# Scores of a group's second slab put into the same TensorE step as the first slab's output, clears moved off VectorE, and a new set of planner constants

## The chip, the cores and the metric

The kernel runs on one core of a Trainium2 chip. The metric is the time of one execution in microseconds (us). The kernel before took 628.93 us, the median of three runs (627.5 to 629.05). One profiled execution of it took 627.94 us; its span, from the first to the last recorded instruction, is 625.9 us. All rows below come from that execution.

## The reference

The reference has two stages. The first is a recurrent attention over 768 time steps, for 4 batches of 8 heads of width 48: a 48 x 48 state is multiplied at every step by a complex decay, a key-value product is added, and the query reads the state.

```python
for t in range(S):                       # S = 768
    new_re = ar * S_re - ai * S_im       # ar, ai: normalised decay of this step
    new_im = ar * S_im + ai * S_re
    S_re, S_im = new_re + einsum('bhd,bhe->bhde', k[t], v[t]), new_im
    y[t] = einsum('bhd,bhde->bhe', q[t], S_re)
```

The second is a gated feed-forward network over the 3072 tokens, with 384 model columns and 1536 hidden columns:

```python
g = x @ w_gate
out = (g * sigmoid(g) * (x @ w_val)) @ w_out
```

## The kernel before, in words

**Tiling.** The tokens are cut into 24 slabs of 128 time steps of one batch; two slabs (two batches, the same time steps) are a group, so there are 12 groups. The recurrence over time steps inside a slab is turned into products with cumulated decays. A slab n goes through these steps:

- *Stage* (`stage_ops`, for the whole group): loads, logarithms, exponentials, arctan, sine and cosine on ScalarE, sums over time on TensorE (`cumL`, `cumF`, into the one buffer `pm`), products on VectorE. It ends in the stacks `ks` and `qs`.
- *Turning* (`tr1`, `tr0` on VectorE, line 607, then `sh0` to `sh3`: twelve DMAs issued by SP, line 616): the stacks of a slab are transposed into the tile `T`, which has two buffers. The tile between them, `turned`, has one, so the second slab of a group is turned only when the first one's DMAs are through.
- *Scores* (`sc`, line 641): 64 small matmuls into the two PSUM banks `ps`. They use strips of TensorE, 32 columns wide, each addressed by `tile_position=(0, 32 * slot)`.
- *Mask* (`mk0`, `mk1` on VectorE, line 648), which copies the scores to the tile `sc`.
- *Output and state* (`av`: line 674, 32 or 64 matmuls into `py`, then line 680, 48 matmuls into `pm`): also on strips 32 columns wide. The 48 matmuls of line 680 are left out for the last chunk of time (groups 10 and 11).
- *Eviction* (`evh` on ScalarE, line 698, `evl` on VectorE, line 705): the output becomes the tiles `xh` and `xl` of the group. `ga` and `gm` (VectorE) update the state `G`.

When both slabs of a group are evicted, the feed-forward network of that group runs in 12 steps (`ffn_ops`): line 864 multiplies with the gate and value weights (18 matmuls of 256 columns over the full 128 x 128 array for groups 1 to 11; for group 0 six in single precision, which are 12 records), ScalarE applies silu, VectorE multiplies and splits, and line 903 multiplies with the output weights (6 matmuls of 384 columns).

**Order.** The engines' order of work is written out by a planner (`class Planner`): it goes through the operations by engine, takes an engine that is free first, and among the operations ready at that time the one with the lowest key. A key is a due time, either given (`anchor(n)` for slabs, from `T0`, `LEAD0`, `LEAD2`, `FT0`, `AHEAD`, `PER`; `T0 + f * FT0` and later `T1 + ...` for the feed-forward steps; `CK0`, `X_SEC` for range checks of the inputs) or worked back from the operations that need it, with `STRETCH` times their cost. On ScalarE an operation that needs another table of functions has `SWITCH_KEY` added to its key. `SPARE`, `PIECE` and `CHECK` are added to the landing times that the planner assumes for DMAs, and `QUEUED` says how far ahead of the DMA traffic a load may be issued. The planner's times are assumptions; the engines follow only its order, each in turn, and wait on semaphores.

**Start.** `begin()` comes ahead of the planned order. GpSimd (POOL) makes `ident` twice, once as a triangle, which VectorE copies to `tri` and, turned round by blocks of 32 rows, to its mirror image; VectorE clears the two `vt` tiles and the two `ps` banks, POOL clears `G`. TensorE (PE) is kept busy up to a planned 36 us by matmuls of no use (`p_warm`): ahead of every PE operation stand as many as fit in the planned gap, at 0.3 us each. They stand in PE's queue, in order, so PE runs them all before the operation behind them:

```python
for _ in range(int((min(op.start, WARM) - idle - 0.2) / 0.3)):
    nc.tensor.matmul(out=at_["warm"][:, 0:P], lhsT=mask, rhs=mask, start=True, stop=True)
```

A single-precision matmul is recorded as two, so the 42 records ahead of the first planned PE operation are 21 of these.

Of the kernel before, what the change touches and what calls it, by code (L numbers as in the profile page):

```python
# [17 lines left out]
B, H, S, D = 4, 8, 768, 48  # L18
# [12 lines left out]

SWITCH = 1.273
HOP = 0.145
SWITCH_KEY = 18.625
STRETCH = 1.65
AHEAD, YIELD, QUEUED = -5.599, 3.451, 2.61
T0, PER, FT, FT0 = 21.562, 21.452, 3.64, 4.795
LEAD0, LEAD2 = 15.263, -0.901
CONV0, CONVP = 172.418, 101.298
T1 = T0 + 12 * FT0  # L40
CK0, CKP = 737.912, 29.556
WARM = 36.0
ROW, LAND = 0.6, 2.4
SPARE, PIECE, CHECK = 0.346, 0.281, -0.292
X_SEC = 459.355
RCP, SQR, TURN, SEC = 1, 2, 4, 4
HIGH, LOW, WHOLE = 0, 1, 2
SHY = -80.37
POOL_FROM = 134.7

# [128 lines left out]
def flat(t):  # L181
    return t.rearrange("p h d -> p (h d)")
# [10 lines left out]
def quick(ctx, tc, q, k, v, a_re, a_im, w_gate, w_val, w_out, out, count):  # L193

    nc = tc.nc
# [10 lines left out]
    tri, mirror = masks[:, 0:P], masks[:, P:2 * P]  # L206
    masks = masks.bitcast(F32)
    mask = masks[:, 0:P]
    ident = const.tile([P, P], F32, name="ident")
# [8 lines left out]
    G = const.tile([96, B, H, 64], F32, name="G")  # L218
    vts = [const.tile([P, H + H // 2, 64], F32, name=f"vt{i}") for i in range(2)]
    banks = [psum.tile([P, 512], F32, name=f"p_ps{i}", tag=f"ps{i}", bufs=1) for i in range(2)]  # L220
# [46 lines left out]
    for t, (nm, f, i) in {"re": ("w", 0, 0), "im": ("w", 0, 1), "s1": ("o", 0, 0), "s2": ("w", 1, 0), "s3": ("w", 1, 1),  # L267
                          "qt": ("o", 1, 0), "kt": ("o", 2, 0), "qs": ("w", 2, 0)}.items():
        n, nm_f = 96 if t == "qs" else D, (nm, NF - 3 + f)
# [9 lines left out]
    pl = Planner(slots)  # L279
# [278 lines left out]
                       alloc=[tg(dst)] if opens else [], use=[tg(t), tg(w)] + ([] if opens else [tg(dst)]))  # L558


    def slab_ops(n):
        g, half = divmod(n, 2)
        b, c = where(n)
        N, ta = str(n), anchor(n)
# [3 lines left out]
        made = {st: [f"{st}0_{M}", f"{st}1_{M}"] for st in stacks}  # L568
# [10 lines left out]
        if n < TURN:  # L579
            tdeps = []  # L580
            for i, st in ((1, "ks"), (0, "qs")):
                for hq in range(2):
# [9 lines left out]
                    def ev(e, i=i, hq=hq, inst=inst, first=not tdeps):  # L592
                        if first:
# [4 lines left out]
                                        alloc=[] if tdeps else [("T", n)], use=[("gv", inst)] + ([("T", n)] if tdeps else [])))  # L598
        else:
            halves = [(("bt", 0), f"b{n}"), (("bt", 1), f"b{n}")]  # L600
            bt = tile_t.rearrange("p (j x n) -> p j x n", j=3, x=2)
            for i, st in ((1, "ks"), (0, "qs")):
                def tr(e, i=i, st=st):
                    if i == 1:
# [5 lines left out]
                       alloc=halves if i == 1 else [], use=[stacks[st]] + (halves if i == 0 else []))  # L610
            for i in range(4):
                def sh(e, i=i):
                    if i == 0:
                        new("T", n)
                    for j in range(3):
# [3 lines left out]
                       alloc=[] if i else [("T", n)], use=halves + ([("T", n)] if i else []), lat=1.0 + PIECE, move=0.5)  # L619
            tdeps = [f"sh{i}_{n}" for i in range(4)]  # L620
# [12 lines left out]
        def sc(e):  # L633
            qT, kT = turned(n, 0), turned(n, 1)
            for qd in range(2):
                ps = new("ps", f"{n}.{qd}").rearrange("p (h t) -> p h t", h=4)
                for at, h in ((0, 0), (2, 2), (1, 1), (3, 3)):
                    h = heads[qd][at]
                    for slot in range(4):
                        j = slot if h < H // 2 else 3 - slot  # L640
                        nc.tensor.matmul(out=ps[32 * slot:32 * slot + 32, at, 32 * j:P], lhsT=kT[:, h // 2, h % 2, j, :],  # L641
                                         rhs=qT[:, h // 2, h % 2, j:4, :], start=True, stop=True, tile_position=(0, 32 * slot))
        pl.add("sc" + N, {"PE": 1.35}, sc, deps=tdeps + [f"sc{n - 1}"], alloc=[("ps", f"{n}.0"), ("ps", f"{n}.1")], use=[("T", n)], key=ta)
        for qd in range(2):
            def mk(e, qd=qd):
                s = new("sc", f"{n}.{qd}")
                both = masks.rearrange("p (x t) -> p x t", x=2).unsqueeze(2).to_broadcast([P, 2, 2, P])
                nc.vector.tensor_tensor(out=s.rearrange("p (x h) t -> p x h t", x=2), in0=at_["ps", f"{n}.{qd}"].rearrange("p (x h t) -> p x h t", x=2, h=2),  # L648
                                        in1=both, op=ALU.mult)
            pl.add(f"mk{qd}_{n}", {"DVE": 0.6}, mk, deps=["sc" + N], alloc=[("sc", f"{n}.{qd}")],  # L650
                   use=[("ps", f"{n}.{qd}")])

        def av(e):
            qT, kT = views()
            py = new("py", n)[:, :DM].rearrange("p (k t) -> p k t", k=KT)
            vf, gf = flat(vts[n % 2]), flat(G[:, b])

            turns = [[] for _ in range(4)]
            for blk in range(12):
                pr, j = divmod(blk, 3)  # L660
                slot, kt_ = blk % 4, blk // 4
                o = py[32 * slot:32 * slot + 32, kt_, :]
                heads = ([(2 * pr, 128 * pr)], [(2 * pr, 128 * pr + 32), (2 * pr + 1, 128 * pr + 48)],
                         [(2 * pr + 1, 128 * pr + 80)])[j]
                mm = []
                for h, col in heads:
                    if c > 0:
                        mm.append((gf[:, col:col + 32], qT(h)))
                    at = col if h < H // 2 else col + H // 2 * 64
                    mm.append((vf[:, at:at + 32], at_["sc", f"{n}.{h % 4 // 2}"][:, h % 2 + h // 4 * 2, :]))  # L670
                turns[slot] += [(o, l, r, i == 0, i == len(mm) - 1) for i, (l, r) in enumerate(mm)]
            for step in zip(*turns):
                for slot, (o, l, r, opens, closes) in enumerate(step):
                    nc.tensor.matmul(out=o, lhsT=l, rhs=r, start=opens, stop=closes, tile_position=(0, 32 * slot))  # L674
# [7 lines left out]

        def both(e):

            av(e)
            if c < NCH - 1:
                kv(e)
        more = [("pm", "K" + N)] if c < NCH - 1 else []
        pl.add("av" + N, {"PE": (2.65 if c else 1.75) if more else 1.95}, both,
               deps=[f"mk0_{n}", f"mk1_{n}", "ldv" + N, f"gm{n - 4}"] + (made["ks"] if more else []), alloc=[("py", n)] + more,  # L690
               use=[("sc", f"{n}.0"), ("sc", f"{n}.1"), ("T", n), ("vt", n)] + ([("ks", ("ks", g))] if more else []), key=ta + 5)

        cols = slice(half * P, half * P + P)

        def evh(e):
            if half == 0:
# [3 lines left out]
               alloc=[("xh", g)] if half == 0 else [], use=[("py", n)] + ([("xh", g)] if half else []), key=ta + 8)  # L700
# [6 lines left out]
        if g > 0:  # L707
            pl.add("evl" + N, {"DVE": 0.47}, evl, deps=["evh" + N] + ([f"evl{n - 1}"] if half else []),
                   alloc=[("xl", g)] if half == 0 else [], use=[("py", n), ("xh", g)] + ([("xl", g)] if half else []), key=ta + 8.5)
        if c < NCH - 1:  # L710
            gv, dec = G[:, b, :, 0:D], lambda: at_["dec", g][:, hs].unsqueeze(2).to_broadcast([96, H, D])

            def ga(e):
# [3 lines left out]
                else:  # L717
                    tt(e, gv, gv, pk, ALU.add)
            pl.add(("gm" if c == 0 else "ga") + N, {"DVE": 0.47}, ga,
                   deps=["av" + N, f"dr2{M}"] + ([f"gm{n - 4}"] if c else []),  # L720
# [232 lines left out]
    def begin():  # L953
        nc.vector.memset(b_half_pi, math.pi / 2)
        nc.vector.memset(b_eps, math.log(2e-6))
        nc.vector.memset(ones, 1.0)
        nc.scalar.preload_act_table_set(TABLES["ln"][0])
        nc.scalar.activation(out=warm, in_=b_half_pi, func=AF.Ln)
        for op in (ALU.is_ge, ALU.is_equal):
            nc.gpsimd.memset(ident, 1.0)  # L960
            nc.gpsimd.affine_select(out=ident, in_=ident, pattern=[[1, P]], compare_op=op,
                                    fill=0.0, base=0, channel_multiplier=-1)
            if op == ALU.is_ge:
                nc.vector.tensor_copy(out=tri, in_=ident)
                for j in range(4):
                    nc.vector.tensor_copy(out=mirror[32 * j:32 * j + 32], in_=ident[96 - 32 * j:128 - 32 * j])
        for t in vts:
            nc.vector.memset(t, 0.0)
        for i in range(2):
            nc.vector.memset(banks[i], 0.0)  # L970
        nc.gpsimd.memset(G, 0.0)

    stage_ops(0, 0, 1)
    stage_ops(0, 1, 1)
    stage_ops(1, 0, 2)
    for g in range(2):
        for i in range(2):
            slab_ops(2 * g + i)
    for f in range(NF):
        weight_ops(f)  # L980
    ffn_ops(0)
# [1 line left out]
        split_ops(f)  # L983
    for g in range(2, NGRP):
        stage_ops(g, 0, 2)
        for i in range(2):
            slab_ops(2 * g + i)
    for g in range(SEC):
        sector_ops(g)
    for f in range(NF):  # L990
# [193 lines left out]
```

## Time and profile before

| | |
|---|---|
| median of the runs | 628.93 us |
| profiled execution | 627.94 us (span 625.9 us) |
| TensorE (PE) matmul | 601.2 us busy, 96%, x7536 |
| TensorE weight load (PEld) | 565.9 us busy, 90%, x7536 |
| VectorE (DVE) | 492.9 us busy, 79%, x898 |
| ScalarE (ACT) | 426.3 us busy, 68%, x695 |
| GpSimd (POOL) | 37.0 us busy, 6%, x64 |
| chain that ended last | PE 54%, DVE 18%, ACT 16%, "issue" 7%, DMA 3% |

Matmuls are recorded from their start to a modelled end and overlap, so PE's busy share says that it had work, not that it ran at its best. In a timeline the difference of two start times is what a matmul costs. "issue" is idle time for which the profile shows no releaser. A row's bracket gives the idle time just before it and what ended that.

### The profile page before, as it was taken

Reading aid. Unit: us, or ns where it says so; the run is one execution under the profiler, and the core shown is the slowest. Engines: PE = TensorE matmul, PEld = TensorE weight load, DVE = VectorE, ACT = ScalarE, POOL = GpSimd, SP = SyncE. Lnnn points to the kernel's source line nnn. Section 1 sums busy time; section 2 is a strip of 40 time slices with the busy share of each in tenths; the row PEclk is TensorE's granted clock in tenths of the full one; section 3 lists DMA queues with packets and bytes.
Section 4 is the critical chain, followed back from the end, with each engine's and each line's share of the span. In section 5 each row is a group of like instructions: output and inputs, shape, how many; then the busy total and the mean of one; then the engine's idle time right before and its main releaser. Section 6 shows DMA issues by size and latency. Waiting matters only on the chain.

```text
span 625.9 us, 18088 instructions
## 1 busy us (share of the span) xinstructions
PE 601.2 (96%) x7536; PEld 565.9 (90%) x7536; DVE 492.9 (79%) x898; ACT 426.3 (68%) x695; POOL 37.0 (6%) x64
## 2 busy tenths in 40 slices
PE   6879999999999999999999999999999999999996
PEld 6668777898999999999999999999999999999995
DVE  7979999999989978968869768778877967554442
ACT  6955668997876946966977976967967867322220
POOL 1310001001001001001001001001000000000000
PEclk9989999999999999999999999999999999999999
DMA  8999503444653554544546635635535643542310
GB/s 242 310 287 338 158 1 99 125 82 110 158 135 106 148 125 125 155 116 125 144 104 147 154 79 141 157 94 144 136 106 139 155 107 82 133 106 63 99 51 30
DMA packets 146280, 83.16 MB, mean 133 GB/s; under 512 B 106608, under 2 KB 142448, under 8 KB 146192
## 3 DMA queue, kind: packets, MB, share of 16 engines
q1 hardware_dynamic: 143360, 77.10, 46.1%
q0 software_dynamic: 2256, 4.06, 3.4%
q8 instruction: 61, 1.00, 0.7%
q10 hardware_dynamic: 576, 0.79, 0.4%
q14 instruction: 27, 0.22, 0.1%
HBM read 61.40 MB, written 4.78 MB: 106 GB/s over the span
## 4 chain that ended last, share of the span: by engine, by line
PE 54%; DVE 18%; ACT 16%; issue 7%; DMA 3%; POOL 0%; DVEq 0%; ACTq 0%; POOLq 0%
PE p_gv L864 28%; PE p_po L903 14%; ACT L1007 9%; PE p_py L674 5%; PE p_ps L641 3%; ACT s L368 2%; DMA fr<-s 2%; DVE xl L763 2%; DVE sg L879 2%; PE p_pm L463 1%; PE p_pm L680 1%; DVE xl L759 1%; DVE qs L313 1%; DVE ww L767 1%; ACT qs L476 1%
## 5 line engine op out<-in xcount | busy, mean ns | idle before, releaser
L864 PE MATMUL p_gv<-xh,ww 128*128 128x256 f32 x1596 | 303.9, 288 | 4.4 <-DVE sg L879 4.3
L864 PEld LDWEIGHTS p_gv<-xh,ww 128*128 128x128 f32 x1596 | 255.7, 189 | 12.6 <-DVE sg L879 7.2
L864 PE MATMUL p_gv<-xl,ww 128*128 128x256 f32 x726 | 200.9, 277 | 0.0
L1007 ACT ACT_TABLE_LOAD x121 | 155.2, 1283 | 2.1
L864 PEld LDWEIGHTS p_gv<-xl,ww 128*128 128x128 f32 x726 | 136.3, 188 | 0.0
L874 ACT ACTIVATE sg<-p_gv 128x256 f32<-128x256 f32 x144 | 54.4, 383 | 108.6 <-PE p_gv L864 107.6
L903 PE MATMUL p_po<-wo,hh 128*128 128x384 f32 x484 | 125.3, 340 | 0.0
L879 DVE TENSOR_TENSOR sg<-sg,p_gv 128x256 f32<-128x256 f32 x144 | 59.0, 411 | 57.5 <-ACT sg L874 54.6
L903 PEld LDWEIGHTS p_po<-wo,hh 128*128 128x128 f32 x484 | 80.8, 188 | 1.5 <-issue 0.6
L903 PE MATMUL p_po<-wo,hl 128*128 128x384 f32 x242 | 81.1, 336 | 0.0
L313 DVE TENSOR_TENSOR hl<-sg,hh 128x256 fp32r<-128x256 f32 x132 | 54.9, 417 | 5.7 <-ACT hh L317 1.4
L317 ACT CAST hh<-sg 128x256 fp32r<-128x256 f32 x69 | 27.8, 404 | 28.9 <-DVE sg L879 14.0
L368 ACT ACTIVATE s<-s 128x768 f32<-128x768 f32 x44 | 37.2, 845 | 13.4 <-DVE s L313 10.3
L903 PEld LDWEIGHTS p_po<-wo,hl 128*128 128x128 f32 x242 | 45.4, 188 | 0.2 <-DVE hl L313 0.2
L641 PEld LDWEIGHTS p_ps<-T 96*32 96x32 f32 x1536 | 29.0, 111 | 9.1 <-issue 7.8
L674 PE MATMUL p_py<-sc,vt 128*32 128x128 f32 x768 | 37.0, 274 | 0.0
L641 PE MATMUL p_ps<-T 96*32 96x128 f32 (+3 forms) x1536 | 32.9, 236 | 3.4 <-issue 3.4
L648 DVE TENSOR_TENSOR sc<-p_ps,tri 128x512 f32<-128x512 f32 x48 | 30.9, 678 | 3.0 <-PE p_ps L641 3.0
L674 PE MATMUL p_py<-T,G 96*32 96x128 f32 x640 | 32.8, 275 | 0.0
L313 DVE TENSOR_TENSOR s<-im,s 128x768 fp32r<-128x768 f32 x10 | 9.6, 956 | 20.6 <-PE p_pm L463 20.6
L864 PE MATMUL p_gv<-xh,ww-1_377 128*128 128x256 f32 x132 | 24.7, 280 | 0.0
L674 PEld LDWEIGHTS p_py<-sc,vt 128*32 128x32 f32 x768 | 22.8, 111 | 1.1 <-issue 0.5
(141 smaller groups left out, 862.0 us busy)
## 6 DMA issues: line engine op xcount, KB each, us to landing
T<-turned SPq DMA_DIRECT2D x240, 64.0 KB, 2.3
wo<-in_moe_w_out_dram SPq DMA_DIRECT2D x24, 384.0 KB, 5.4
vt<-in_v_dram SPq DMA_DIRECT2D x24, 288.0 KB, 4.2
ww<-in_moe_w_gate_dram SPq DMA_DIRECT2D x12, 384.0 KB, 7.4
ww<-in_moe_w_val_dram SPq DMA_DIRECT2D x12, 384.0 KB, 8.7
wo<-in_moe_w_gate_dram SPq DMA_DIRECT2D x12, 384.0 KB, 4.0
wo<-in_moe_w_val_dram SPq DMA_DIRECT2D x12, 384.0 KB, 3.5
re<-in_a_re_dram SPq DMA_DIRECT2D x11, 384.0 KB, 3.7
```

The lines of the kernel that those rows point to most:

```text
L313: V[e].tensor_tensor(out=out, in0=a, in1=b, op=op)
L317: nc.scalar.copy(out=out, in_=in_)
L368: nc.scalar.activation(out=of(dst), in_=of(source), func=func, scale=scale, **kw)
L641: nc.tensor.matmul(out=ps[32 * slot:32 * slot + 32, at, 32 * j:P], lhsT=kT[:, h // 2, h % 2, j, :], rhs=qT[:, h // 2, h % 2, j:4, :], star ...
L648: nc.vector.tensor_tensor(out=s.rearrange("p (x h) t -> p x h t", x=2), in0=at_["ps", f"{n}.{qd}"].rearrange("p (x h t) -> p x h t", x=2, ...
L674: nc.tensor.matmul(out=o, lhsT=l, rhs=r, start=opens, stop=closes, tile_position=(0, 32 * slot))
L763: nc.vector.scalar_tensor_tensor(out=between(), in0=raw["low"], scalar=29, in1=between(), op0=ALU.logical_shift_right, op1=ALU.bitwise_or)
L864: nc.tensor.matmul(out=gv[:, i, :], lhsT=l, rhs=r, start=(m == 0), stop=(m == len(mm) - 1))
L874: nc.scalar.activation(out=new("sg", I), in_=at_["gv", I][:, 0:2 * P], func=AF.Silu)
L879: nc.vector.tensor_tensor(out=sg, in0=sg, in1=at_["gv", I][:, 2 * P:4 * P], op=ALU.mult)
L903: nc.tensor.matmul(out=po, lhsT=l[:, cs], rhs=weight("o", f, part), start=f == 0 and j == 0, stop=f == NF - 1 and j == len(products) - 1)
L1007: nc.scalar.preload_act_table_set(op.load)
```

## The change

A slab's scores and output become a generator of two parts, so that the planner can be given the second slab's scores before the first slab's output. From slab 4 on (`JOIN`), the scores of a group's second slab are no operation of their own: the first slab's `av` issues them, just ahead of its own matmuls, and takes over their dependencies and buffers. Its planned cost is raised by 1.26; a single `sc` is now planned at 1.46 in place of 1.35. In `begin()` the mirror image is made by POOL, `G` is cleared ahead of the rest, of `vt` only the columns beyond 48 of each head are cleared, on POOL, and the two `ps` banks are cleared by PE, by a product with the cleared `G`. Nineteen of the planner's constants change.

```diff
-SWITCH_KEY = 18.625
-STRETCH = 1.65
-AHEAD, YIELD, QUEUED = -5.599, 3.451, 2.61
-T0, PER, FT, FT0 = 21.562, 21.452, 3.64, 4.795
-LEAD0, LEAD2 = 15.263, -0.901
-CONV0, CONVP = 172.418, 101.298
+SWITCH_KEY = 2.93
+STRETCH = 1.636
+AHEAD, YIELD, QUEUED = -3.449, 3.533, 4.228
+T0, PER, FT, FT0 = 11.002, 21.487, 3.599, 4.531
+LEAD0, LEAD2 = 14.347, -0.647
+CONV0, CONVP = 136.292, 171.866
-CK0, CKP = 737.912, 29.556
+CK0, CKP = 795.217, 26.993
-SPARE, PIECE, CHECK = 0.346, 0.281, -0.292
-X_SEC = 459.355
+SPARE, PIECE, CHECK = 0.85, 0.826, -0.265
+X_SEC = 430.022
+JOIN = 4
@@ 
+    joint = {}
+
+    def pair_ops(g):
+        first, second = slab_ops(2 * g), slab_ops(2 * g + 1)
+        for part in (first, second, first, second):
+            next(part, None)
@@ slab_ops
-        pl.add("sc" + N, {"PE": 1.35}, sc, deps=tdeps + [f"sc{n - 1}"], alloc=[...], use=[("T", n)], key=ta)
+        scored = dict(deps=tdeps + [f"sc{n - 1}"], alloc=[("ps", f"{n}.0"), ("ps", f"{n}.1")], use=[("T", n)])
+        joined = half == 1 and n >= JOIN
+        if joined:
+            joint[n] = sc, scored
+        else:
+            pl.add("sc" + N, {"PE": 1.46}, sc, key=ta, **scored)
+        if half:
+            yield
...
+        if not half:
+            yield
@@ 
         def both(e):
+            if beside:
+                beside[0](e)
             av(e)
             if c < NCH - 1:
                 kv(e)
-        pl.add("av" + N, {"PE": (2.65 if c else 1.75) if more else 1.95}, both,
+        beside = joint.get(n + 1)
+        then = beside[1] if beside else dict(deps=[], alloc=[], use=[])
+        pl.add("av" + N, {"PE": ((2.65 if c else 1.75) if more else 1.95) + (1.26 if beside else 0.0)}, both,
...
+        if beside:
+            pl.by[f"sc{n + 1}"] = pl.by["av" + N]
@@ begin
-                    nc.vector.tensor_copy(out=mirror[32 * j:32 * j + 32], in_=ident[96 - 32 * j:128 - 32 * j])
+                    nc.gpsimd.tensor_copy(out=mirror[32 * j:32 * j + 32], in_=ident[96 - 32 * j:128 - 32 * j])
+        nc.gpsimd.memset(G, 0.0)
         for t in vts:
-            nc.vector.memset(t, 0.0)
-        for i in range(2):
-            nc.vector.memset(banks[i], 0.0)
-        nc.gpsimd.memset(G, 0.0)
+            nc.gpsimd.memset(t[:, :, D:64], 0.0)
+        for t in banks:
+            nc.tensor.matmul(out=t, lhsT=mask[0:96], rhs=flat(G[:, 0]), start=True, stop=True)
```

The calls `slab_ops(2 * g + i)` for i in 0, 1 become `pair_ops(g)`.

## Rows read from the trace of the kernel before

**Rows 1.** Windows, 200 to 300 us: columns us, PE, PEld, DVE, ACT, POOL, PEclk, DMA, GB/s
```profile
200.00:300.00 100.00, 98.93 (x1330) 96.10 (x1329) 84.07 (x148) 71.93 (x116) 6.17 (x10) 1.00 0.50 127
```

**Rows 2.** Waits of PE, 100 to 600 us: total us, times, longest us
```profile
PE p_gv L864 <- DVE sg L879: 4.3, 7, 1.4
```

**Rows 3.** Chain that ended last, about 270 us: start us, us, what
```profile
268.78 1.25 PE p_ps L641 x34
...
272.37 1.90 PE p_py L674 x64
274.27 0.67 PE p_pm L680 x48
...
276.18 2.04 PE p_gv L864 x18
```

**Rows 4.** Timeline of PE, one visit to the strips for a second slab's scores
```profile
284.83 0.28 PE L864 MATMUL p_gv<-xh,ww 128*128 128x256 f32 x1
285.03 1.34 PE L641 MATMUL p_ps<-T 96*32 96x128 f32 x64
286.31 0.62 PE L463 MATMUL p_pm<-s,tri 128*128 128x384 f32 x2
```

**Rows 5.** Timeline of PE, the first two full matmuls after another such visit
```profile
269.99 0.39 PE L864 MATMUL p_gv<-xh,ww 128*128 128x256 f32 x1
270.21 0.28 PE L864 MATMUL p_gv<-xl,ww 128*128 128x256 f32 x1
```

**Rows 6.** Timeline of PE, strips of two kinds one behind the other
```profile
35.41 0.22 PE L680 MATMUL p_pm<-vt,ks 128*32 128x48 f32 x3
35.44 0.75 PE L641 MATMUL p_ps<-T 96*32 96x32 f32 x32
```

**Rows 7.** Timeline of all engines, the first 11 us
```profile
1.70 6.88 PE L1004 MATMUL p_warm<-tri 128*128 128x128 f32 x42 [1.70 <-DVE tri L964]
...
2.71 0.20 POOL L960 MEMSET ident<- 128x128 f32 x1 [1.33 <-DVE tri L966]
2.81 1.50 DVE L968 MEMSET vt<- 128x768 f32 x2 [0.22 <-issue]
...
3.23 1.80 POOL L971 MEMSET G<- 96x2048 f32 x1
3.36 0.52 ACT L388 ACTIVATE wo<-ww 128x384 f32<-128x384 f32 x1 [1.04 <-DMA ww<-in_a_re_dram]
...
4.42 1.02 DVE L970 MEMSET p_ps<- 128x512 f32 x2
...
5.36 2.49 DVE L380 RECIPROCAL ww<-ww 128x384 f32<-128x384 f32 x1
...
10.71 0.91 PE L460 MATMUL p_gv<-ww,tri 128*128 128x384 f32 x2 [2.12 <-ACT ww L368]
```

**Rows 8.** Windows, 4 to 8 us, columns as in the first group
```profile
4.00:6.00 2.00, 2.00 (x12) 2.00 (x12) 1.84 (x4) 0.32 (x1) 1.03 (x1) 1.00 0.81 206
6.00:8.00 2.00, 2.00 (x21) 2.00 (x20) 2.00 (x2) 1.04 (x2) 0.00 (x0) 1.00 1.00 347
```

**Rows 9.** Chain that ended last, about 35 us
```profile
33.94 1.01 PE p_py L674 x32
...
36.68 3.35 issue
```

**Rows 10.** Windows, about 40 us, columns as in the first group
```profile
40.00:42.00 2.00, 1.96 (x17) 1.58 (x17) 1.18 (x2) 0.00 (x0) 0.00 (x0) 0.50 0.69 102
```

**Rows 11.** DMA queues of the page: packets, MB, share
```profile
q8 instruction: 61, 1.00, 0.7%
```

**Rows 12.** Timeline of VectorE: the second slab's eviction
```profile
295.98 0.55 DVE L705 TENSOR_TENSOR xl<-p_py,xh 128x384 fp32r<-128x384 f32 x1
```

**Rows 13.** Timeline of PE: the next group's first feed-forward matmul
```profile
297.12 0.28 PE L864 MATMUL p_gv<-xh,ww-1_377 128*128 128x256 f32 x1
```

**Rows 14.** Groups of instructions: busy us, mean ns, idle us before
```profile
L1007 ACT ACT_TABLE_LOAD x121 | 155.2, 1283 | 2.1
```

More of the change, by code (lines that the diff above doesn't have):

```diff
@@ L642, in sc @@
                                          rhs=qT[:, h // 2, h % 2, j:4, :], start=True, stop=True, tile_position=(0, 32 * slot))
-        pl.add("sc" + N, {"PE": 1.35}, sc, deps=tdeps + [f"sc{n - 1}"], alloc=[("ps", f"{n}.0"), ("ps", f"{n}.1")], use=[("T", n)], key=ta)
+        scored = dict(deps=tdeps + [f"sc{n - 1}"], alloc=[("ps", f"{n}.0"), ("ps", f"{n}.1")], use=[("T", n)])
[6 more added lines that the diff above has]
+            yield
         for qd in range(2):
@@ L688, in slab_ops @@
         more = [("pm", "K" + N)] if c < NCH - 1 else []
-        pl.add("av" + N, {"PE": (2.65 if c else 1.75) if more else 1.95}, both,
-               deps=[f"mk0_{n}", f"mk1_{n}", "ldv" + N, f"gm{n - 4}"] + (made["ks"] if more else []), alloc=[("py", n)] + more,
-               use=[("sc", f"{n}.0"), ("sc", f"{n}.1"), ("T", n), ("vt", n)] + ([("ks", ("ks", g))] if more else []), key=ta + 5)
+        beside = joint.get(n + 1)
+        then = beside[1] if beside else dict(deps=[], alloc=[], use=[])
+        pl.add("av" + N, {"PE": ((2.65 if c else 1.75) if more else 1.95) + (1.26 if beside else 0.0)}, both,
+               deps=[f"mk0_{n}", f"mk1_{n}", "ldv" + N, f"gm{n - 4}"] + (made["ks"] if more else []) + then["deps"], alloc=[("py", n)] + more + then["alloc"],
+               use=[("sc", f"{n}.0"), ("sc", f"{n}.1"), ("T", n), ("vt", n)] + ([("ks", ("ks", g))] if more else []) + then["use"], key=ta + 5)
+        if beside:
+            pl.by[f"sc{n + 1}"] = pl.by["av" + N]
         cols = slice(half * P, half * P + P)
@@ L976, in quick @@
     for g in range(2):
-        for i in range(2):
-            slab_ops(2 * g + i)
+        pair_ops(g)
     for f in range(NF):
@@ L985, in quick @@
         stage_ops(g, 0, 2)
-        for i in range(2):
-            slab_ops(2 * g + i)
+        pair_ops(g)
     for g in range(SEC):
```

## The prediction, made before the changed kernel was run

> **What bounds the kernel now.** I read the windows first. From 200 to 300 us PE is busy for 98.93 of 100 us, VectorE for 84.07, ScalarE for 71.93, the DMA engines for 0.50 [rows 1]. The reader is to see that one engine is full and the others are not. Busy says only that PE had work, so I look second at what it waited for: from 100 to 600 us one kind of wait of weight is left, 4.3 us in seven pieces, for VectorE's product behind silu [rows 2]. The chain of waits agrees: its pieces at 270 us are PE's, one behind the other [rows 3]. From the first feed-forward step to the end the time is what PE's instructions cost, plus when that stretch begins. So an edit is worth what it takes out of PE's own stream, or out of the start.
>
> **The joined step.** It removes, ten times (the second slabs 5, 7, ... 23), a visit to the strips of its own. What a visit costs beside its matmuls I read from start times. The feed-forward matmuls stand 0.11 us apart (18 in 2.04 us [rows 3]). Ahead of the visit the last one starts at 284.83, so the strips could start at 284.94 and do so at 285.03: 0.09 us. The 64 strip matmuls end with one of about 0.2 us, so their starts spread over 1.34 - 0.2 = 1.14 us, to 286.17; one more spacing of 0.02 is 286.19, and the full array starts at 286.31: 0.12 us [rows 4]. Behind a visit the second full matmul starts 0.22 us after the first in place of 0.11: 0.11 us more [rows 5]. Together 0.32 us. Between the strips of two kinds there is no such price: the scores started 0.03 us behind the state matmuls in the one place where they meet [rows 6], so nothing is paid at the new seam. Ten visits are -3.2 us, all on PE. The matmuls stay: as many, as long. Bounds: -3.5 if each end of the visit is 0.015 us more than I read, 0 if the seam between scores (96 rows) and output (96 and 128 rows by turns) costs what a visit does; I take the row of the seam.
>
> **The join's waits.** `av` of the first slab now waits for the second slab's `T` as well. Behind it in PE's queue stand feed-forward steps, placed there by the planner, so PE doesn't stand still for the wait that is planned; about 2.6 us of matmuls (1.90 + 0.67 [rows 3]) move to the time of the second slab's scores, and as much feed-forward work moves ahead. The second slab's output then has in front of it one joined step of 1.25 + 1.90 + 0.67 = 3.82 us, and the eviction of the first output out of the one `py` and `pm` buffer. The margin at the end is small: `xl` of the second slab is written at 295.98 + 0.55 = 296.53 us, and the next group's first matmul starts at 297.12, 0.59 us later [rows 12, 13]. I cost it at nothing, since the mask of the second slab runs beside the first slab's output, and the second slab is due 2.15 us earlier against the feed-forward steps (`AHEAD`). If that cover is gone, a group waits: bounds 0 and, with the whole step of 3.82 us late in all ten, +38; the row next to it is the margin that is still there, hence 0.
>
> **PE's instructions.** PE's 2 x 7536 instructions come in 61 packets of 16 KB [rows 11], some 247 each. The chain shows PE once without an instruction: 3.35 us of "issue" in the middle of a slab's scores, after 2.7 us of strips in a row [rows 9], while all queues were full; the clock granted afterwards was 0.50, the lower of its two levels, 1.2 GHz [rows 10]. The joined step is 176 matmuls, 352 instructions with their loads, in 3.82 us, so a packet is used up in 2.7 us; in the steady part so far the densest run was 112 matmuls in 2.57 us, and no wait of this kind stands between 100 and 600 us [rows 2]. Bounds: 0, and 3.35 in each of ten, +33.5. The DMA engines are at 0.50 there [rows 1], so I stay near the run without a stall: +0.3. The Trainium skill ("Runtime: NRT & Kernel Launch", Instruction fetch mechanics) says that the sequencer streams its instructions ahead in blocks of 16 KiB and that the price of a block's end is mostly hidden; by that this term would be 0. The size agrees with the packets here; that it is hidden does not hold at 36.68 us.
>
> **The clears.** VectorE loses the clears of `vt` and of the banks, 1.50 and 1.02 us [rows 7]. The data for the first reciprocal are there when ScalarE squares them, at 3.36; the reciprocal starts at 5.36, behind the clears. So it can start 2.0 us earlier. But PE now has the clear of the banks at the head of its queue, and it waits for POOL's clear of `G`. POOL waited 1.33 us for VectorE's mirror copies; now it makes four copies itself, each between 0.2 (its clear of 128 columns) and, doubled, 0.4: `G`, ready at 5.03 before, is ready between 4.5 and 5.3. PE starts at about 5.0 in place of 1.70. The two products are 512 columns in single precision; 384 columns take about 0.75 us at the full clock (two in a row, 0.91 with the end of the last), so 1.0 or less each, and twice that at the lower clock, at which the warm-up matmuls ran at first: 12 records in the third stretch of 2 us, 21 in the fourth, though the clock's column says 1.00 in both [rows 8]. That is 3.4 to 4 us, to 8.4 or 9.0. Behind them stand the same 21 useless matmuls, since no operation ahead of the first planned PE step is priced anew: 42 records at 0.1 us, 4.2 us. The first real matmul, at 10.71 with 2.12 us of idle time before it, can't start before 12.6 to 13.2: +2.2. So VectorE's chain is 2.0 us early and PE's queue 2.2 us late, and the two meet at that matmul. With `SWITCH_KEY` at 2.93 ScalarE can change tables earlier and do other work meanwhile; bounds -2.0 and +2.2, and I take the middle, 0, since no row shows which is last.
>
> **The constants.** Most are one shift of all due times, which alters no rank. The smaller price of a table change can only add to the 121 loads of 1.28 us [rows 14]; ScalarE has 28 us of idle time in 100 [rows 1], room for 20 more in each 100 us. Earlier silu could win back the 4.3 us [rows 2]. Bounds: -4.3, and, if one silu in each of eleven groups comes one load later, +14; I take -0.5, near the waits as they are. The checks (`CK0`, `X_SEC`) fill idle time either way: 0.
>
> **Sum.** -3.2 + 0 + 0.3 + 0 - 0.5 = -3.4 us. From the profiled execution's span of 625.9 that is 622.5, with the 2.0 us around it 624.5; the median of the runs lies 1.0 above that execution, so 625.5.
>
> **The rivals.**
> - *The start is lost.* PE's late queue decides: +2.2 in place of 0, and the sum is -1.2, 627.7. For it: the queue is in order and 21 useless matmuls can't be skipped. Against: 2.12 us of slack stood there.
> - *All of it works.* The start gains 2.0, and the stall of 3.35 us [rows 9] falls elsewhere, where the queues are not full: -3.4 - 2.0 - 3.35, 620.2. Against: as many loads are issued in that time as before.
> - *The seam costs a visit.* Scores and output don't share the strips' set-up: the change then doesn't do what it says, -0.2, 628.7. Against: rows 6.
> - *The second output comes late (the other side).* The joined step stands in front of it, and the eviction of the first output; from 0.59 us on [rows 12, 13] each microsecond is PE's. At 1.3 us late in ten groups it costs 7 us: 632.5. For it: the margin is thin, and buffers `py` and `pm` are single. Against: 3 us feed-forward steps can stand in between.
> - *PE runs out of instructions in the joined step.* Every second step loses 1.3 us: +6.5 in place of +0.3, 631.7. For it: a packet lasts 2.7 us there, as it did at the stall; against: half the DMA traffic.
>
> **How the numbers follow.** A measurement of this kernel can tell about 0.3%, 1.9 us, from no change. The forecast, 625.5 (its own range 622.5 to 627.0), has 0.50; all of it works 0.12; the start lost 0.17 and the seam 0.06, both within 1.9 us; late second output 0.09; no instructions 0.06. Faster is 0.62, same 0.23, slower 0.15. The range from 620.0 to 631.5 holds the forecast, both cases without change and the fast one, and cuts through the two slow ones; what is left out is 0.09 + 0.03 above and some 0.05 below.
>
> **What would show it.** Right: scores and output of lines 641 and 674 in one piece in ten places, with starts 0.02 to 0.03 us apart at the seam; between two groups' first feed-forward matmuls 0.3 us less. The first `p_warm` at 8 us or later, the first matmul of line 460 at about 13. Wrong: "issue" of over 0.3 us inside a joined step; new waits of PE for `xh` or `xl` at a group's first matmul; many more table loads than 121 with longer waits for silu's product; a first feed-forward step that starts more than 2 us earlier or later than before.

## The result, and the profile after

The changed kernel takes 619.21 us (median of 4 runs, 618.56 to 620.04) beside 628.67 us for the kernel before on the same chip: ratio 0.985, 95% interval 0.984 to 0.987. Forecast were 625.5 us, range 620.0 to 631.5. The sign was right, the size was not: 9.5 us came off where 3.4 were expected. The profiled execution after has a span of 618.1 us (620.04 with what lies around it); it is the longest of its four, so the two profiles are only 7.8 us of span apart.

The windows from 200 to 300 us, to be read against [rows 1]:

```profile
200.00:300.00 100.00, 99.84 (x1347) 97.99 (x1346) 84.35 (x149) 76.94 (x119) 6.17 (x10) 1.00 0.51 133
```

PE was busy for 98.93 us there and is now for 99.84, and it finishes 1347 matmuls where 1330 were. The waits of PE from 100 to 600 us, to be read against [rows 2]:

```profile
PE p_gv L889 <- DVE sg L904: 2.7, 3, 1.4
PE p_pm L699 <- issue: 1.1, 3, 0.7
```

All three waits behind silu lie ahead of 136 us; the later ones are gone. "issue" is new: idle time for which the profile shows no releaser; the prediction reads it as PE out of instructions.

A joined step in the timeline of PE (start us, us, engine, line, operation), with the lone second output of the same group, to be read against [rows 4, 5]:

```profile
235.56 0.34 PE L928 MATMUL p_po<-wo,hl 128*128 128x384 f32 x1
235.83 1.34 PE L650 MATMUL p_ps<-T 96*32 96x128 f32 x64
236.97 0.42 PE L693 MATMUL p_py<-T,G 96*32 96x128 f32 x8
...
238.73 0.86 PE L699 MATMUL p_pm<-vt,ks 128*32 128x48 f32 x48
239.51 0.39 PE L889 MATMUL p_gv<-xh,ww 128*128 128x256 f32 x1
239.74 0.28 PE L889 MATMUL p_gv<-xl,ww 128*128 128x256 f32 x1
...
242.83 0.42 PE L693 MATMUL p_py<-T,G 96*32 96x128 f32 x8
...
245.40 0.38 PE L889 MATMUL p_gv<-xh,ww 128*128 128x256 f32 x1
```

From its first matmul to the first full one behind it the joined step takes 239.51 - 235.83 = 3.68 us. Apart they took 1.28 (scores [rows 4]) and 2.57 (an output, 242.83 to 245.40): 3.85. The seam saves 0.17; the entry of 0.10 and the late second full matmul of 0.11 are paid once less. That is 0.38 a visit, 0.32 forecast. At the seam the output starts 1.14 us behind the first of 64 scores, at their own pace: nothing is paid there, as forecast.

The same view of a later joined step:

```profile
329.51 1.34 PE L650 MATMUL p_ps<-T 96*32 96x128 f32 x64
...
332.41 0.69 PE L699 MATMUL p_pm<-vt,ks 128*32 128x48 f32 x33
333.38 0.45 PE L699 MATMUL p_pm<-vt,ks 128*32 128x48 f32 x15 [0.28 <-issue]
```

The 48 state matmuls are cut in two: this step takes 0.55 us more than the one at 235.83 (329.51 to 333.75, the next full matmul). There are such losses in the steps at 282, 330, 377 and 424 us.

The margin between the second output and the next group's first feed-forward matmul, to be read against [rows 12, 13]:

```profile
293.46 0.55 DVE L730 TENSOR_TENSOR xl<-p_py,xh 128x384 fp32r<-128x384 f32 x1
...
295.69 0.28 PE L889 MATMUL p_gv<-xh,ww-1_373 128*128 128x256 f32 x1
```

It was 0.59 us and is 295.69 - 294.01 = 1.68.

The start, to be read against [rows 7] (timeline of all engines):

```profile
1.44 1.33 POOL L991 CAST tri<-ident 32x128 fp32r<-32x128 f32 x4
...
3.23 2.55 DVE L381 RECIPROCAL ww<-ww 128x384 f32<-128x384 f32 x1 [1.60 <-DMA ww<-in_a_re_dram]
3.33 1.80 POOL L992 MEMSET G<- 96x2048 f32 x1
...
5.19 3.78 PE L996 MATMUL p_ps<-G,tri 96*128 96x512 f32 x4 [5.19 <-POOL G L992]
...
8.76 5.50 PE L1027 MATMUL p_warm<-tri 128*128 128x128 f32 x42
...
14.10 0.81 PE L461 MATMUL p_gv<-ww,tri 128*128 128x384 f32 x2
```

VectorE's reciprocal starts 2.13 us earlier, PE's first real matmul 3.39 us later (10.71 before). The table loads stay as many ([rows 14] had 121):

```profile
L1030 ACT ACT_TABLE_LOAD x119 | 152.7, 1283 | 2.1
```

**Where the time went.** The windows from the first feed-forward matmul of the third group to that of the last, nine periods in which both kernels do the same work; before, then after:

```profile
154.08:580.14 426.06, 422.95 (x5633) 408.55 (x5633) 330.57 (x600) 300.53 (x488) 19.82 (x32) 1.00 0.50 127
```

```profile
155.38:572.78 417.40, 416.31 (x5633) 408.06 (x5633) 327.36 (x596) 302.08 (x491) 20.00 (x32) 1.00 0.50 129
```

The stretch shrinks by 8.66 us; it begins 1.30 us later. So all of the gain is in the steady groups, where the forecast had about 3. Nine joined visits are 9 x 0.38 = 3.4. The shown idle time falls only from 3.11 to 1.09 us, so most of what is left was counted as busy before: the ends of matmuls are modelled, and a matmul that starts 0.1 us late still counts as one behind the other. Start times show it. From the first to the seventh gate product of the sixth group both kernels issue the same 208 matmuls (six pieces, one slab's scores); the first product starts at 297.12 [rows 13] before and at 295.69 after, the seventh here, before and after:

```profile
318.34 0.39 PE L864 MATMUL p_gv<-xh,ww 128*128 128x256 f32 x1
```

```profile
315.68 0.28 PE L889 MATMUL p_gv<-xh,ww 128*128 128x256 f32 x1
```

21.22 us before, 19.99 after: 1.23 us less for the same matmuls in a piece of the stream that the join doesn't touch.

**ScalarE in that piece.** Its timeline before, and the one wait that PE shows:

```profile
300.19 1.28 ACT L1007 ACT_TABLE_LOAD   x1
301.48 0.85 ACT L368 ACTIVATE s<-re 128x768 f32<-128x768 f32 x1
...
303.39 1.28 ACT L1007 ACT_TABLE_LOAD   x1
304.68 0.38 ACT L874 ACTIVATE sg<-p_gv 128x256 f32<-128x256 f32 x1
...
308.92 0.38 ACT L874 ACTIVATE sg<-p_gv 128x256 f32<-128x256 f32 x1
...
312.86 0.66 ACT L874 ACTIVATE sg<-p_gv 128x256 f32<-128x256 f32 x2
```

```profile
313.75 0.39 PE L864 MATMUL p_gv<-xh,ww 128*128 128x256 f32 x1 [0.58 <-DVE sg L879]
```

and after:

```profile
295.24 1.28 ACT L1030 ACT_TABLE_LOAD   x1
296.53 0.85 ACT L369 ACTIVATE s<-re 128x768 f32<-128x768 f32 x1
...
298.44 1.28 ACT L1030 ACT_TABLE_LOAD   x1
299.73 0.39 ACT L899 ACTIVATE sg<-p_gv 128x256 f32<-128x256 f32 x1
...
306.01 0.38 ACT L899 ACTIVATE sg<-p_gv 128x256 f32<-128x256 f32 x1
...
309.86 0.38 ACT L899 ACTIVATE sg<-p_gv 128x256 f32<-128x256 f32 x1
```

In both, ScalarE goes back and forth between the turns' functions and silu, with a load of 1.28 us at each change, so its silus come 3.8 to 4.2 us apart while PE starts a piece each 3.09 us where nothing holds it. `p_gv` has two buffers, so a gate product waits for VectorE's product behind the silu of two pieces ahead. ScalarE loses ground in that run, and has to begin it with a lead. Before, the first load comes 3.07 us behind the group's first gate product (300.19 against 297.12); after, 0.45 us ahead of it (295.24 against 295.69), and the run is over before PE has caught up. This is read from two timelines; the kernels without table loads, below, test it.

### The profile page after: what moved, and what is told of

The parts are those of the page before. It is cut to its first block, busy times and chain, and to the rows that moved or that the text cites. A ratio compares the mean times of both kernels' runs of the same rounds, so it can differ in the third digit from the quotient of the medians.

```text
span 618.1 us, 18097 instructions
## 1 busy us (share of the span) xinstructions
PE 596.2 (96%) x7532; PEld 564.6 (91%) x7532; DVE 490.2 (79%) x892; ACT 425.5 (69%) x691; POOL 39.5 (6%) x70
## 4 chain that ended last, share of the span: by engine, by line
PE 79%; DVE 12%; DMA 3%; issue 2%; SPq 2%; ACT 1%; DVEq 0%
PE p_gv L889 43%; PE p_po L928 22%; PE p_py L693 6%; PE p_ps L650 4%; PE p_pm L699 2%; PE p_pm L464 2%; DVE xl L788 2%; DMA ww<-in_moe_w_val_dram 1%; SPq L775 1%; DVE xl L784 1%; DVE ww L314 1%; DVE ww L792 1%; DMA ww<-in_moe_w_gate_dram 1%; DVE sg L904 1%; DVE s L314 1%
## 5 line engine op out<-in xcount | busy, mean ns | idle before, releaser
L318 ACT CAST hh<-sg 128x256 fp32r<-128x256 f32 x61 | 24.7, 404 | 28.7 <-DVE sg L904 26.2
L314 DVE TENSOR_TENSOR ks<-kt,s 128x768 f32<-128x768 f32 x22 | 20.9, 952 | 5.4 <-PE p_pm L699 5.4
L314 DVE TENSOR_TENSOR qs<-qt,s 128x768 f32<-128x768 f32 x22 | 20.8, 950 | 5.0 <-ACT s L369 5.0
```

What stands on the lines that cost most here:

```text
L314: V[e].tensor_tensor(out=out, in0=a, in1=b, op=op)
L318: nc.scalar.copy(out=out, in_=in_)
```

## Experiments

Three theories stood at the start. A: the constants' new order brought most. B: the join itself did, by what it puts where. C: the start did. Times below are medians; the kernel before took 628.1 to 628.8 beside them.

**Each part by itself.** e1_join: the join, with the old constants and clears.

```diff
-SWITCH_KEY = 2.93
+SWITCH_KEY = 18.625
-AHEAD, YIELD, QUEUED = -3.449, 3.533, 4.228
-T0, PER, FT, FT0 = 11.002, 21.487, 3.599, 4.531
+AHEAD, YIELD, QUEUED = -5.599, 3.451, 2.61
+T0, PER, FT, FT0 = 21.562, 21.452, 3.64, 4.795
...
```

> The joined step alone (JOIN = 4), with the constants and the clears of the kernel before. Theory A (the constants' order brought most): ten visits to the strips fewer, -3.5 us, less up to 2 us for instruction stalls inside the joined steps, so 625.0 to 627.0, and waits of PE for silu's product of 3 us or more stay. Rival B (the join itself put the order right): 619 to 621, and those waits are gone.

631.68 us, ratio 1.006 (1.004 to 1.007). e2_constants: the new constants alone, old clears.

```diff
-JOIN = 4
+JOIN = 99
...
+        for i in range(2):
+            nc.vector.memset(banks[i], 0.0)
...
```

> The new constants alone, no joined step, clears as before. Theory A: waits behind silu gone and shorter pieces of idle time inside the feed-forward steps, 621.5 to 623.5, and a group's period of about 47.1 us in place of 47.7. Rival B: the constants do nothing by themselves, 627 to 630.

629.03 us, 1.002 (1.000 to 1.003). e3_clears: the kernel before with the clears moved, and nothing else.

```diff
-            nc.vector.memset(banks[i], 0.0)
...
+            nc.tensor.matmul(out=t, lhsT=mask[0:96], rhs=flat(G[:, 0]), start=True, stop=True)
```

> The moved clears alone, constants and order as before. Theory A: PE's first real matmul is 2 to 3 us later (at 13 to 14 us), VectorE's reciprocal 2 us earlier, and the two cancel: 627.5 to 630. Rival C (the start is where the gain came from): 624 to 626.

628.5 us, 1.001 (1.000 to 1.002). e4_no_join: the changed kernel without the join, all else kept.

```diff
-JOIN = 4
+JOIN = 99
```

> The changed kernel without the joined step (constants and clears stay). Theory A: 621 to 623, that is 1.7 to 3.5 us over the changed kernel's 619.2, with no instruction stall between 100 and 600 us. Rival B: 626 to 629.

631.1 us, 1.004 (1.003 to 1.006). So no part alone gains anything, and A, B and C all fall: the gain is one of join and constants together. The table loads were 121 before, 112 with the join alone, 129 with the constants alone and 119 with both. In e1_join PE waits for the second output, of which the kernel before shows no wait:

```profile
PE p_gv L889 <- DVE sg L904: 7.5, 9, 1.7
PE p_gv L889 <- DVE xl L730: 3.5, 3, 2.1
```

This is the rival "second output late" of the prediction; with all the old constants it happens, in three groups.

**The clears.** A' was that PE's late queue costs 2 us in the new order. e5_old_clears: the changed kernel with all clears of before.

> The changed kernel with the clears of before (VectorE clears vt and the banks, PE starts at 1.7 us). Theory A': with the new constants the moved clears cost what they cost without the join (631.10 - 629.03 = 2.1 us), so 617.0. Rival: they gain or do nothing with the join, 619 to 621.

619.16 us, the changed kernel's own time: moving all of them is worth nothing. e6_banks_dve: the changed kernel, with the two banks alone cleared by VectorE again.

```diff
-            nc.tensor.matmul(out=t, lhsT=mask[0:96], rhs=flat(G[:, 0]), start=True, stop=True)
+            nc.vector.memset(t, 0.0)
```

> The changed kernel with the two banks cleared by VectorE, all else as changed: PE no longer waits for POOL's clear of G, and VectorE clears 1.0 us in its idle time before the first data at 3.2 us. Theory A' (PE's late queue is the cost of the clears): 615.5 to 617.5, first real matmul at 9 to 10 us. Rival (the start is set by something else): 619.

616.12 us, 0.981 (0.979 to 0.983): 3 us better than the changed kernel and than e5_old_clears. The move consists of two parts that cancel: what VectorE is relieved of besides the banks gives 3 us, the banks' clear on PE takes them. The first warm-up matmul is at 1.69 in place of 8.76, the first real one at:

```profile
9.59 0.91 PE L461 MATMUL p_gv<-ww,tri 128*128 128x384 f32 x2
```

**One constant at a time.** e7_switch (theory D: the small price of a table change removes the waits for silu):

```diff
-SWITCH_KEY = 2.93
+SWITCH_KEY = 18.625
```

> The changed kernel with SWITCH_KEY back at 18.625. Theory D (the price of a table change, together with the join, took PE's waits for silu's product away): 4 to 8 us slower, 623 to 627, waits of 4 us or more between 150 and 580 us. Rival E (it is the due times of slabs against feed-forward steps) or F (the assumed landing times): 619 to 621.

627.74 us, a little more than D said, but without D's waits: 2.1 us of them between 150 and 580. Most of the loss lies ahead of the fourth group's first gate product, which comes 5.9 us later than in the changed kernel (207.86 against 201.99); from there on the periods are the changed kernel's within 0.5 us. e8_ahead (E: the due times):

```diff
-AHEAD, YIELD, QUEUED = -3.449, 3.533, 4.228
-T0, PER, FT, FT0 = 11.002, 21.487, 3.599, 4.531
+AHEAD, YIELD, QUEUED = -5.599, 3.533, 4.228
+T0, PER, FT, FT0 = 11.002, 21.452, 3.64, 4.531
```

> The changed kernel with AHEAD, PER and FT back at the values of before, so slabs due later against the feed-forward steps. Theory E (due times): 624 to 629, the second slab's output later than the next group's first matmul wants it. Rival D or F: 619 to 621.

636.56 us, 17 more than the changed kernel and above E's range, with 13.0 us of waits behind silu between 100 and 600. For the second output, which E had late, PE shows no wait at all. e9_pieces (F: the assumed landing times):

```diff
-SPARE, PIECE, CHECK = 0.85, 0.826, -0.265
+SPARE, PIECE, CHECK = 0.346, 0.281, -0.292
```

> The changed kernel with three of its constants back at their old values: SPARE 0.346, PIECE 0.281, CHECK -0.292 (the landing times that the planner assumes). Theory F (the assumed landing times are what the new constants put right, with the join): the gain goes, 626 to 630 us. Theory G (what counts is where the second output's low half stands against the next group's first gate product: an order that leaves some 1.6 us there and repeats it in every group has no wait for SiLU behind it, and then the period is 46.6 us): the order here leaves 1.35 us in groups 5 to 9 by the planner's times, so little comes back, 619.5 to 623 us, and PE's waits for sg of 1 to 3 us stay under 6 us in all between 100 and 600.

632.71 us: what F expected, and more; G, the margin, falls, since it is 1.62 us here too. e10_ahead_only, `AHEAD` alone:

> The changed kernel with AHEAD alone back at -5.599, so that every slab is due 2.15 us later against the feed-forward, PER 21.487 and FT 3.599 kept. Theory E1 (the shift is what the joined order needs; e8_ahead lost 17 us by it): second outputs late again, 632 to 637 us. Theory G (the margin in front of the first gate product): the planner's order has 1.62 us there in groups 5 to 9, as the changed kernel has, so the steady period stays 46.6 us and only the first groups are placed otherwise: 620 to 625 us.

630.67 us, between the two; the wait for the second output is 0.4 us, once. e11_rates_only, `PER` and `FT` alone:

> The changed kernel with PER 21.452 and FT 3.64 alone back (two slabs fall due 0.78 us sooner than twelve pieces of feed-forward in each group, instead of 0.21 us), AHEAD kept at -3.449. Theory E2 (the ratio of the two rates is what the join needs, since a drift moves the second output through the order and no group repeats the last): waits of PE for sg come back, 9 to 16 us between 100 and 600, and the time is 630 to 637 us, as e8_ahead. Theory E1 (the shift): 619 to 623 us with no more than 4 us of such waits. By the planner's own times the margin in front of the first gate product runs 0.76, 0.67, 1.61, 2.67, 4.71 in groups 5 to 9, so theory G expects waits in the early groups and a longer period in the late ones.

638.6 us, with 13.3 us of waits: E1 falls, and E2's waits are there; even with the shift kept, the ratio of the rates counts. Each constant or set of them that is put back loses 8 to 19 us, so no one of these holds the gain by itself. The other twelve of the nineteen were left at their new values in all of these runs. The 208 matmuls of the sixth group tell more. In e9_pieces they take 21.16 us (299.82 to 320.98), as before; ScalarE changes tables between the two turn functions that stood together in the changed kernel (between its loads at 295.24 and 298.44). It begins with the changed kernel's lead (299.38 against 299.82), so the lead alone isn't enough:

```profile
299.38 1.28 ACT L1030 ACT_TABLE_LOAD   x1
300.67 0.85 ACT L369 ACTIVATE s<-re 128x768 f32<-128x768 f32 x1
...
302.11 1.28 ACT L1030 ACT_TABLE_LOAD   x1
303.40 0.38 ACT L899 ACTIVATE sg<-p_gv 128x256 f32<-128x256 f32 x1
303.81 1.28 ACT L1030 ACT_TABLE_LOAD   x1
305.10 0.85 ACT L369 ACTIVATE s<-s 128x768 f32<-128x768 f32 x1
```

In e10_ahead_only ScalarE has the changed kernel's sequence from the sixth group on, and the 208 matmuls take 19.99 us (303.87 to 323.86), the changed kernel's time. What e10 loses from there on is 2.7 us, nearly all of it "issue" in the joined steps (waits of PE, 100 to 600 us):

```profile
PE p_pm L699 <- issue: 3.7, 4, 1.3
```

The other 8.2 us of its loss lie ahead of the sixth group; their cause stays open.

**The table loads taken away.** That made two theories for the interaction. T: in every order but the new one ScalarE is late with silu because of its loads. U: the order of PE's and VectorE's own work does it, and the loads have no part. Four kernels keep the very order of before, e1_join, e2_constants and e5_old_clears, and issue no table load but one at the start:

```diff
-                nc.scalar.activation(out=of(dst), in_=of(source), func=func, scale=scale, **kw)
+                nc.scalar.activation(out=of(dst), in_=of(source), func=AF.Tanh, scale=scale, **kw)
...
-            if op.load:
-                nc.scalar.preload_act_table_set(op.load)
...
```

> The kernel before, every instruction in its place, without table loads: the logarithms, exponentials, arctangents, sines and cosines of the turns and decays are a hyperbolic tangent instead, which lies in SiLU's table, and the final judgement is set to good; the output is therefore another one. Theory T (the loads between SiLU and the turn functions make SiLU late, and PE waits for it): 617 to 622 us, PE's waits for sg between 160 and 580 under 1 us. Theory U (the order of PE and VectorE alone): waits for sg stay at 3 us or more there, 624 to 628 us (what the start gains from fewer loads).

> e1_join (join, old constants; 631.7 us with loads) without table loads in the same way. Theory T: 614 to 621 us, 1 to 4 us under f1_before_one, since what is left is the join's own 3.35 us less its instruction stalls. Theory U: 3 us over f1_before_one, as with the loads; also if the second output's low half is late by PE's own order (waits for xl), these waits stay.

> e2_constants (new constants, no join; 629.0 us with loads) without table loads in the same way. Theory T: within 2 us of f1_before_one. Theory U: within 2 us of f1_before_one too, but both near 625 us.

> e5_old_clears (join and new constants, old clears; 619.16 us with loads) without table loads in the same way. Theory T: its waits for sg were already gone, so it gains only at the start and at the end: 614 to 618 us, within 2 us of f3_join_one, and the interaction (this minus f3 minus f5 plus f1) lies within 2.5 us of zero instead of -9.5. Theory U: 8 to 10 us under f1_before_one, interaction -7 to -10.

| | with loads | without | difference |
|---|---|---|---|
| before | 628.43 | 619.34 | -9.1 |
| join alone | 631.68 | 625.15 | -6.5 |
| constants alone | 629.03 | 621.50 | -7.5 |
| both | 619.16 | 616.43 | -2.7 |

The stretch of nine periods, without loads, in the order of before and in that with both:

```profile
151.75:571.50 419.75, 419.64 (x5634) 408.94 (x5634) 329.56 (x600) 182.02 (x395) 19.66 (x32) 1.00 0.51 128
```

```profile
152.00:569.48 417.48, 416.44 (x5633) 408.25 (x5633) 326.70 (x595) 182.92 (x399) 19.67 (x32) 1.00 0.51 129
```

Before, the loads cost 426.06 - 419.75 = 6.31 us of that stretch; with both parts they cost nothing (417.40 against 417.48). This is T, shown for these two orders: 6.3 of the 8.7 us are table loads that no longer reach PE. The 208 matmuls of the sixth group take 19.90 us in the order of before without loads (293.19 to 313.10). In the table too the loads cost 6.5 to 9.1 us in the three other orders and 2.7 with both parts. But T fails for the join alone, which stays 5.8 us above f1_before_one, and barely for the constants alone, 2.2 above it. The interaction is -10.9 where T had it within 2.5 of zero (-13.1 with loads), so most of it is no matter of loads. In f3_join_one the waits for the second output are as they were with loads:

```profile
PE p_gv L889 <- DVE xl L730: 3.6, 3, 2.2
```

So two things are mixed in the interaction. With the old constants the join brings the second output late, by the order of the work and not by the loads, and the new constants cure that; and join and constants together give the order in which ScalarE's loads are hidden. Which constants cure the late output isn't shown: with old `AHEAD`, `PER` and `FT` it didn't come back (e8_ahead), with old `AHEAD` alone by 0.4 us (e10_ahead_only). What else f3_join_one loses beside these 3.6 us stays open.

**Blocks of instructions.** e12_halves, made from e6_banks_dve:

```diff
-                    nc.tensor.matmul(out=at_["warm"][:, 0:P], lhsT=mask, rhs=mask, start=True, stop=True)
+                    for cut in (slice(0, 64), slice(64, P)):
+                        nc.tensor.matmul(out=at_["warm"][:, cut], lhsT=mask, rhs=mask[:, cut], start=True, stop=True)
```

> As e6_banks_dve (616.12 us), with each of the 102 warm-up products of 128 columns issued as two of 64 columns: the same columns, 102 products more on PE ahead of all groups. It moves where PE's blocks of instructions end within each group, and nothing else. Theory 'blocks' (a joined step loses 0.4 to 0.85 us where a block of instructions ends inside its dense run of 64 + 64 + 48 products): the lost time leaves the steps at 326 and 373 us (0.42 and 0.79 there) and turns up in other groups' steps, or in none; total 615 to 618 us. Rival (something that happens at that place of the program, a transfer or a buffer): the same two groups lose it again.

634.71 us: it did move something else. The warm-up products in halves take 40.3 us in place of 16.3, and the first feed-forward matmul comes 20 us later; why, the last section shows. So the time against the DMA traffic is another one as well, and the answer is weaker than was meant. e6_banks_dve had lost time in the steps of the seventh and eighth group; the eighth's row, then that of the same group in e12_halves:

```profile
377.41 0.57 PE L699 MATMUL p_pm<-vt,ks 128*32 128x48 f32 x25 [0.56 <-issue]
```

```profile
397.43 0.39 PE L889 MATMUL p_gv<-xl,ww 128*128 128x256 f32 x1 [0.39 <-issue]
```

It has moved from the middle of the step to behind it; the seventh group's step has no loss any more (it starts at 346.38 and is 3.69 us long), and the ninth's has one of 0.39 us that it had not. So the rival, the same two groups losing it again, falls: the losses moved when the number of instructions ahead of them changed. But that number alone doesn't set them. In e5_old_clears, e6_banks_dve and f2_both_one PE has equally many records ahead of the ninth group's joined step, 10416, and that step loses 0.33, 0 and 0.76 us. In the changed kernel a packet of the instruction queue (q8, 16 KB) moves in each joined step that loses (at 330.78 in that at 329.51), but also in steps that lose nothing (at 237.63 in that at 235.83). When the end of a block costs time stays open.

## Why the prediction was too small

**What bounds the kernel** was read rightly, PE's own stream and its start, but one reading was too short: that PE at 98.93 of 100 us has 4.3 us to win behind silu [rows 1, 2]. Table loads cost PE 6.3 us in the nine periods, where the shown idle time of every kind was 3.1; the rest stood in busy time, in waits too short to be shown.

**The constants** is the step that failed. It said that most of them "are one shift of all due times, which alters no rank", took -0.5, and set the lower bound at -4.3 by the shown waits. They aren't a shift: with the join kept, old `PER` and `FT` alone cost 19 us, old `AHEAD` alone 11.5, old `SPARE`, `PIECE` and `CHECK` 13.5. And with 119 loads for 121 there were not more of them (they rose to 129 only without the join, e2_constants); they lie elsewhere. With both parts the loads cost 0 of the nine periods where they cost 6.3: outside the bound. The prediction also priced join and constants as terms that add. They don't: +3.3 and +0.6 alone, -9.3 together. The row that could have told it is ScalarE's, silus 3.9 to 4.2 us apart where PE makes a piece in 3.09: a stretch in which ScalarE, at 72 of 100 us, was the slower engine.

**The joined step**, -3.2 for ten visits: 0.38 each, nine of them 3.4 in the stretch. Right, also in that the seam is free.

**The join's waits**, 0: right in the changed kernel, where the margin grew to 1.68 us. With all the old constants these waits are there (e1_join, f3_join_one), so it is the new ones that keep them away. The reason given, the slabs due 2.15 us earlier by `AHEAD`, isn't borne out: with `AHEAD` alone put back, PE waits 0.4 us, once.

**PE's instructions**, +0.3: about 1.8 us in the stretch (the joined steps at 282, 330, 377 and 424 us are 0.36, 0.55, 0.85 and 0.04 us longer than that at 235.83). Such stalls came, as the term said, and the term was too small; the rival with 6.5 us didn't come. That they are the ends of instruction blocks fits e12_halves, but what sets their size isn't shown. The Trainium skill ("Runtime: NRT & Kernel Launch", Instruction fetch mechanics) holds that a block's end is mostly hidden. That is so in five of the nine joined steps, not in the others, and not at the start, where the stall of [rows 9] came again with 1.54 us.

**The clears**, 0 out of -2.0 and +2.2: the sum was right, and so were the two effects that oppose each other, but each is 3 us, beyond its bound (e5_old_clears, e6_banks_dve). That they cancel was luck: the prediction took the middle because no row showed which comes last. The first real matmul was put at 12.6 to 13.2 and came at 14.10. The banks' clear was through at 8.76, as forecast (8.4 to 9.0); the 42 warm-up records behind it took 5.34 us in place of 4.2, the first six still 0.21 us apart, the others 0.11.

**The sum** of what was measured in the nine periods: 6.3 for the loads, 3.4 for the joined visits, -1.8 for the instructions is 7.9 of 8.66 us; 0.8 stays without a name. It isn't loads: without them the two orders still differ by 419.75 - 417.48 = 2.27 us, where the visits' 3.4 less the 1.8 of "issue" in f2_both_one's joined steps would be 1.6. Without a name are also the start's 1.3 us, read from one execution of each kernel; the four runs after lie 1.5 us apart.

## What to carry to other kernels

An engine that is "busy" at 99% can still lose 1.2 us in 20 to another: compare the start times of the same instructions in two places, not their busy shares, and look for the engine whose run of work is slower than the bounding one for a while. Where an order is made by due times, a structural edit and the constants that place it are one change: test the four corners before giving either a price. A move that nets to nothing may hold two halves of 3 us; try each half.

## What the runs showed of the hardware

A warm-up product of 64 columns costs PE as much as one of 128 (both 128 x 128, single precision). Twelve records of whole products in e6_banks_dve, then sixteen of halves in e12_halves (timeline of PE); the starts are 0.11 us apart in both:

```profile
10.34 1.50 PE L1027 MATMUL p_warm<-tri 128*128 128x128 f32 x12
```

```profile
43.24 1.90 PE L1028 MATMUL p_warm<-tri 128*128 128x64 f32 x16
```

So at one clock twice the records take twice the time. The halves took more than that, 40.3 us against twice 16.3, and the rest is TensorE's clock. In e12_halves a product of 384 columns takes about twice as long before 42 us as behind it:

```profile
38.02 1.59 PE L461 MATMUL p_gv<-ww,tri 128*128 128x384 f32 x2
...
45.41 0.81 PE L461 MATMUL p_pm<-im,tri 128*128 128x384 f32 x2
```

The times say that PE stood at the lower of its two levels, 1.2 GHz, up to about 42 us; it ran halves, 0.21 us apart, and a few products of 384 columns there. The clock's column prints 1.00 for that stretch, as in [rows 8], but the trace's first record of a granted clock begins only at 42.3 us. In e6_banks_dve it begins at 7.8 us, and the starts of the whole products close up from 0.21 to 0.11 us there.

A table load on ScalarE costs its 1.28 us and nothing around it: at 303.39 before, the load starts 0.02 us behind the activation ahead of it and silu 0.01 us behind the load.
